# Threshold attention and a SwiGLU block on one core: a weight's conversion in the first batch is parted over two slots, its clamp goes to GpSimd, and the raw places change

## The chip, the cores and the metric

The kernel runs on one core of a Trainium2 chip. The metric is the device time of one execution in microseconds. The engines of the core work side by side, each through a queue of its own in order: PE (TensorE, matmuls), DVE (VectorE), ACT (ScalarE), POOL (GpSimd) and SP (SyncE, which here only issues DMAs). They wait for each other by semaphores.

## What is computed

The reference, cut to what matters:

```python
# q, k, v: (8, 8, 576, 64), tau a scalar
scores = scale * np.matmul(q, k.transpose(0, 1, 3, 2))
thresh = np.max(scores, axis=-1, keepdims=True) - tau
scores = np.where(scores >= thresh, scores, -1000000000.0)
attn = np.exp(scores - np.max(scores, axis=-1, keepdims=True))
attn = attn / (np.sum(attn, axis=-1, keepdims=True) + 1e-09)
x = np.matmul(attn, v)            # then (B,H,S,D) -> (B*S, H*D) = (4608, 512)
g = x @ w_gate                    # (512, 1536)
out = (g * (1 / (1 + np.exp(-g))) * (x @ w_val)) @ w_out
```

The three weights come as 64-bit floats; the kernel makes 32-bit ones of them itself.

## The kernel before, in words

**The stages.** The first batch of the attention is worked on in an order written out by hand (loop of L682): eight segments, each of one pair of heads, first four segments with the tiles 0 and 1 of 128 queries (n = 0 to 3), then four segments with the tiles 2, 3 and 4 (n = 4 to 7; tile 4 is the half tile of 64 queries, and has one maximum, one exponential and one mask instead of two). After it, from `halved` on, come the 7 other batches in slots of a third of a pair of heads; there a planner (`Plan`, with a cost in us for each job and a rank) decides the order on DVE, ACT, POOL and SP, while the order on PE is that of the calls.

**One tile of the first batch.** `scores` is a generator that is stepped from the loop: PE makes the scores (L415, L421), DVE their maxima `nm` (L432), ACT the threshold `th` and the exponential (L435, L436), DVE masks and sums (L439), sums up and inverts (L441, L442 `ri`). Of the two heads of a tile, ACT scales the first (L449) and POOL the second (L447). Between these steps stand the work of the tile before, that is the transposes on PE (L481, L483), their copies on ACT (L489, L493, L496) and the products with v (L513, L516, copy L518), and pieces of the matmuls for the SwiGLU of the first 256 tokens (L530 `pg` and `pv`, with ACT's L545 and L546, DVE's L554 and POOL's product L561). The scores need two PSUM buffers; a tile of two heads takes both, so that the next tile's scores wait for the masks.

**A weight's conversion.** A piece of the weights is 128 x 768 values, 16 pieces of `w_gate` with `w_val` and 8 of `w_out`. SP fetches its raw 64-bit words into a place (L277, L280); there are six places of 6 KB a partition: 0 to 3 in `wo`, 4 in `xall`, 5 in `extra`. Then ACT takes the magnitude of the upper word into the weight's own place (L296) and the lower word into one of three buffers `lo` that take turns (L297); a clamp (L289) follows, a shift by 3 (L310), on DVE the sign by a XOR with the raw upper word (L313, `SCALAR_TENSOR_TENSOR`), and on POOL the addition of `lo` (L315). After L313 and L297 the raw place may be fetched into again. The clamp is on POOL for what is split in the segments n = 0 to 3 (`early_slots`), and on DVE later. In a tile, `split_weights` stands before the masks and `join_weights` (clamp, shift, XOR and addition of the piece split one tile earlier) after `ri`. In the half tile of n = 4 to 6 (`double`), two pieces are joined and a second one is split. `need(n)` forces conversions that a matmul needs at once.

**Where the results lie.** The eight pieces of `w_out` are written into `wo`, on which the places 0 to 3 lie too: the pieces 0 and 1 lie on place 0, the pieces 2 and 3 on place 1, and so on.

**What is left.** The pieces that are not through at the end of the first batch go to the planner by `rest_of_weights` (ACT L834 and L837, DVE L842, L844, L846, POOL L848, SP L825). In the slots, `FIRST_POOLED` says how many scalings POOL does of a slot (L1737 in place of ACT's L1740), and `FIRST_MAX_BY_ACT` in which slots ACT instead of DVE exchanges the halves of the maxima (L1701 in place of L1695).

Of the kernel before, what the change touches and what calls it, by code (L numbers as in the profile page):

```python
# [14 lines left out]
ALU = mybir.AluOpType  # L15
# [97 lines left out]
def kernel(  # L113
# [135 lines left out]
    places = [land[:, n * 2 * TW:(n + 1) * 2 * TW] for n in range(NF * DM // (2 * TW))]  # L249
    places += [xall[:, 3 * XW:3 * XW + 2 * TW], extra[:, 4 * S:4 * S + 2 * TW]]  # L250
    assert 2 * TW == 3 * HW and 4 * S + 3 * TW == 3 * WS and 4 * S + TW == 6 * HW
# [5 lines left out]
    nf = TW // DM2  # L257
    wplaces = deque([1, 4, 2, 5, 3, 4, 5, 4])
    for e in range(2):
# [23 lines left out]
    def words(place, dst, w):  # L283
        return places[place].bitcast(U32).rearrange("p (m n w) -> p m n w", m=dst.shape[1], w=2)[:, :, :, w]

    early_slots, clamped = [True], []

    def clamp(eng, x):
        eng.tensor_scalar(out=x, in0=x, scalar1=1.875 * 2.0 ** -80, scalar2=2.0 ** -111, op0=ALU.min, op1=ALU.max)  # L289

    def split_weights():
        if fetched:
            dst, place = fetched.popleft()
            lo = los[0].rearrange("p (m n) -> p m n", m=dst.shape[1])
            los.rotate(1)
            nc.scalar.activation(dst, words(place, dst, 1).bitcast(F32), AF.Abs, scale=2.0 ** -96)  # L296
            nc.scalar.activation(lo, words(place, dst, 0), AF.Identity, bias=minus2, scale=-2.0 ** -51)  # L297
            if early_slots[0]:
                clamp(nc.gpsimd, dst)
                clamped.append(dst)  # L300
            split.append((dst, place, lo))

    def join_weights(n=1):
        steps = [split.popleft() for _ in range(min(n, len(split)))]
        for up, place, lo in steps:
            if not any(up is x for x in clamped):
                clamp(nc.vector, up)
        for up, place, lo in steps:
            ub = up.bitcast(U32)
            nc.vector.tensor_scalar(out=ub, in0=ub, scalar1=3, scalar2=None, op0=ALU.logical_shift_left)  # L310
        for up, place, lo in steps:
            ub = up.bitcast(U32)
            nc.vector.scalar_tensor_tensor(out=ub, in0=words(place, up, 1), scalar=0x80000000, in1=ub,  # L313
                                           op0=ALU.bitwise_and, op1=ALU.bitwise_xor)
            nc.gpsimd.tensor_tensor(out=ub, in0=ub, in1=lo.bitcast(U32), op=ALU.add)  # L315
            joined.append(up)
            used.discard(place)

    def need(n):
        while len(joined) < n:  # L320
            fetch_weights(2)
            if not split:
                split_weights()
            join_weights()
            split_weights()
# [233 lines left out]
    def gates():  # L559
        for ht, gt in ungated:  # L560
            nc.gpsimd.tensor_tensor(out=ht, in0=ht, in1=gt, op=ALU.mult)  # L561
        ungated.clear()
# [115 lines left out]
    for n, seg in enumerate(segs[:2 * NP]):  # L678
# [3 lines left out]
        for x, t in enumerate(seg["tiles"]):  # L682
            go = scores(seg, t)
            next(go)
            if not n and not x:
                run_idle(6)
# [14 lines left out]
            if n or x:  # L701
                split_weights()
                fetch_weights(2)
            next(go)
            double = t == NT and NP <= n < NP + 3
            if more and not double:
                join_weights()
            fill(part)
            next(go)
            fill(part)  # L710
            if double:
                join_weights(2)
                split_weights()
                fetch_weights(2)
            gates()
# [19 lines left out]

    fill(left[0])
    gates()

# [75 lines left out]
    def rest_of_weights():  # L814
# [3 lines left out]
        done, joins = {}, []  # L818
        for dst, srcs, place, lo in todo:
            m = dst.shape[1]  # L820
            j = None
            if srcs:
                def fetch(dst=dst, srcs=srcs, place=place):
                    to = places[place].bitcast(U64).rearrange("p (m n) -> p m n", m=nf)
                    nc.sync.dma_start(out=to, in_=srcs[0])  # L825

                j = job("SP", 0.1, fetch, done.get(place), lag=5.0)
            if lo is None:
# [9 lines left out]

                j = job("ACT", 0.93, up_part, j, done.get(place), rank=2)
                j = job("ACT", 1.03, lo_part, j, before, rank=2)  # L840
            ub = dst.bitcast(U32)
            j = job("DVE", 0.6, lambda dst=dst: nc.vector.tensor_scalar(  # L842
                out=dst, in0=dst, scalar1=1.875 * 2.0 ** -80, scalar2=2.0 ** -111, op0=ALU.min, op1=ALU.max), j, rank=2)
            j = job("DVE", 0.6, lambda ub=ub: nc.vector.tensor_scalar(  # L844
# [1022 lines left out]
    MAX_BY_ACT = (0, 3, 5, 6, 8, 9, 10)  # L1867
    FIRST_POOLED = {1: 3, 2: 2, 3: 2, 4: 3, 5: 1, 7: 2, 8: 2, 9: 1, 10: 2, 11: 1, 12: 1, 13: 3, 15: 3, 16: 3, 18: 3, 19: 1, 20: 1, 21: 3, 22: 1, 23: 3}
    FIRST_MAX_BY_ACT = (1, 2, 3, 6, 9, 12, 14, 15, 16, 17, 18, 20, 21, 22)
    CD = {0: 1, 1: 1, 9: 2, 10: 2, 11: 2}  # L1870
# [151 lines left out]
```

## Time and profile before

| | |
|---|---|
| median of 5 runs | 1377.68 us (1377.41 to 1378.21) |
| profiled execution, its own time | 1377.02 us |
| its span, first to last instruction | 1374.9 us |
| granted TensorE clock | 1.00 throughout |
| PE busy | 1355.7 us, 99% of the span, 15630 matmuls |
| DVE busy | 1076.3 us, 78% |
| ACT busy | 874.4 us, 64% |
| POOL busy | 708.7 us, 52% |

The profile is of one execution; times in it count from the first instruction of the span, and the profiled execution's own time is 2.1 us longer than its span. A row of the timeline has the start, the length, the engine, the line, the operation and in brackets the idle time ahead of it with what ended it. A busy PE is not PE at its peak, since a matmul that stands in the queue with its weights loaded counts as busy.

### The profile page before, as it was taken

Reading aid. Unit: us, or ns where it says so; the run is one execution under the profiler, and the core shown is the slowest. Engines: PE = TensorE matmul, PEld = TensorE weight load, DVE = VectorE, ACT = ScalarE, POOL = GpSimd, SP = SyncE. Lnnn points to the kernel's source line nnn. Section 1 sums busy time; section 2 is a strip of 40 time slices with the busy share of each in tenths; the row PEclk is TensorE's granted clock in tenths of the full one; section 3 lists DMA queues with packets and bytes.
Section 4 is the critical chain, followed back from the end, with each engine's and each line's share of the span. In section 5 each row is a group of like instructions: output and inputs, shape, how many; then the busy total and the mean of one; then the engine's idle time right before and its main releaser. Section 6 shows DMA issues by size and latency. Waiting matters only on the chain.

```text
span 1374.9 us, 39287 instructions
## 1 busy us (share of the span) xinstructions
PE 1355.7 (99%) x15630; PEld 1117.5 (81%) x15630; DVE 1076.3 (78%) x2822; ACT 874.4 (64%) x2278; POOL 708.7 (52%) x656
## 2 busy tenths in 40 slices
PE   9988999999999999999999999999999999999998
PEld 6766787778778778887888888878887788999998
DVE  6788988887887776787678877877777776787786
ACT  6887766676756767767776766776667764330330
POOL 3566498844474669534974288436943593000000
PEclk9999999999999999999999999999999999999999
DMA  8744413465523541555154523553065404423421
GB/s 176 198 134 136 87 36 100 130 181 143 174 51 123 145 114 41 170 143 143 29 159 129 147 55 123 140 144 94 27 196 148 112 20 143 161 78 138 154 69 32
DMA packets 208295, 162.33 MB, mean 118 GB/s; under 512 B 166128, under 2 KB 180464, under 8 KB 202736
## 3 DMA queue, kind: packets, MB, share of 16 engines
q1 hardware_dynamic: 203920, 158.86, 40.5%
q8 instruction: 124, 2.03, 0.6%
q10 hardware_dynamic: 4192, 0.95, 0.3%
q14 instruction: 59, 0.48, 0.1%
HBM read 138.28 MB, written 21.50 MB: 116 GB/s over the span
## 4 chain that ended last, share of the span: by engine, by line
PE 90%; DVE 4%; ACT 3%; SPq 2%; issue 1%; DMA 1%; ACTq 0%; DVEq 0%
PE pb L954 18%; PE pa L954 12%; PE px L1434 12%; PE sc L1666 10%; PE xa L1763 9%; PE pe L954 9%; PE po L1230 5%; PE py L1443 5%; PE sc L1115 2%; PE pg L1161 2%; PE pv L1161 2%; SPq L344 1%; PE pe L1115 1%; PE sc L1434 1%; PE pv L530 1%
## 5 line engine op out<-in xcount | busy, mean ns | idle before, releaser
L1714 DVE SCALAR_TENSOR_TENSOR pall<-sc,th,pall 128x288 f32<-128x288 f32 x504 | 243.7, 514 | 63.1 <-ACT pall L1712 48.9
L954 PE MATMUL pb<-xall,big 128*128 128x256 f32 x1152 | 273.6, 380 | 0.0
L1712 ACT ACTIVATE pall<-sc,nm 128x288 f32<-128x288 f32 x504 | 231.6, 497 | 34.6 <-DVE pall L1714 34.3
L954 PEld LDWEIGHTS pb<-xall,big 128*128 128x128 f32 x1152 | 216.4, 190 | 31.0 <-issue 2.2
L1742 DVE STREAM_TRANSPOSE pall<-pall 128x576 f32<-128x576 f32 x252 | 189.9, 765 | 59.2 <-ACT pall L1740 42.6
L1740 ACT ACTIVATE pall<-pall,ri 128x288 f32<-128x288 f32 x408 | 186.6, 527 | 25.0 <-DVE ri L1728 24.3
L809 POOL TENSOR_TENSOR hall<-hall,tmp 128x512 f32<-128x512 f32 x80 | 103.6, 1295 | 159.7 <-DVE hall L1007 144.3
L954 PE MATMUL pa<-xall,big 128*128 128x256 f32 x768 | 183.4, 382 | 0.0
L954 PEld LDWEIGHTS pa<-xall,big 128*128 128x128 f32 x768 | 143.1, 190 | 22.0 <-issue 3.1
L1666 PE MATMUL sc<-kT,qT 64*32 64x144 f32 (+1 forms) x5376 | 149.5, 346 | 3.0 <-DVE pall L1714 2.2
L1687 DVE TENSOR_REDUCE mx<-sc 128x2 f32<-128x576 f32 x168 | 124.7, 742 | 27.2 <-PE sc L1666 26.7
L1666 PEld LDWEIGHTS sc<-kT,qT 64*32 64x32 f32 x5376 | 98.4, 106 | 56.4 <-issue 20.8
L954 PE MATMUL pe<-xall,big 128*128 128x256 f32 x576 | 137.3, 381 | 0.0
L1763 PE MATMUL xa<-pall,vall 64*32 64x288 f32 x4032 | 132.2, 404 | 1.0 <-DVE hall L1007 0.8
L1737 POOL TENSOR_SCALAR pall<-pall,ri 128x288 f32<-128x288 f32 x96 | 95.7, 1009 | 63.4 <-DVE ri L1728 63.3
L954 PEld LDWEIGHTS pe<-xall,big 128*128 128x128 f32 x576 | 108.5, 190 | 16.9 <-issue 2.7
L1763 PEld LDWEIGHTS xa<-pall,vall 64*32 64x32 f32 x4032 | 76.4, 107 | 50.1 <-issue 7.2
L1722 ACT COPY sums<-sums 32x6 f32<-32x6 f32 x336 | 66.6, 198 | 45.1 <-DVE pall L1714 40.5
L1701 ACT COPY mx<-mx 32x6 f32<-32x6 f32 x196 | 38.1, 194 | 61.2 <-DVE mx L1689 59.2
L1006 ACT ACTIVATE vall<-tmp 128x512 f32<-128x512 f32 x96 | 60.1, 629 | 23.3 <-POOL tmp L809 9.6
L1443 PE MATMUL py<-wo,hall 128*128 128x256 f32 x336 | 74.8, 379 | 0.0
L1689 DVE TENSOR_REDUCE mx<-sc 128x1 f32<-128x288 f32 x168 | 74.6, 444 | 0.0
(257 smaller groups left out, 2471.5 us busy)
## 6 DMA issues: line engine op xcount, KB each, us to landing
big<-sums_hbm SPq DMA_DIRECT2D x42, 1024.0 KB, 5.2
big<-sums_hbm SPq DMA_DIRECT2D x48, 768.0 KB, 4.7
vall<-in_v_dram SPq DMA_DIRECT2D x112, 144.0 KB, 3.0
out_dram<-big SPq DMA_DIRECT2D x32, 256.0 KB, 3.1
qT<-in_q_dram SPq DMA_DIRECT2D x112, 72.0 KB, 4.6
kT<-in_k_dram SPq DMA_DIRECT2D x112, 72.0 KB, 2.9
wo<-in_moe_w_gate_dram SPq DMA_DIRECT2D x16, 384.0 KB, 3.7
wo<-in_moe_w_val_dram SPq DMA_DIRECT2D x16, 384.0 KB, 4.6
```

The lines of the kernel that those rows point to most:

```text
L809: return lambda: nc.gpsimd.tensor_tensor(out=out, in0=a, in1=b, op=op)
L954: nc.tensor.matmul(ps[:, i], w[:, k_, i * P:(i + 1) * P], x[:, k_, :], start=first and i == k_ == 0, stop=True, skip_group_check=True)
L1434: nc.tensor.matmul(ps, a[:, f, :], ws[n][:, f, :], start=bank_ not in begun, stop=True, skip_group_check=True)
L1443: nc.tensor.matmul(ps(), a[:, f, i * P:(i + 1) * P], operands[o][:, f, :], start=first and f == 0, stop=True, skip_group_check=True)
L1666: nc.tensor.matmul(pss[h][(slice(g * G, (g + 1) * G), *part)], qT[hs, col:col + G], kT[hs, c * SH + keys[0]:c * SH + keys[1]], start=True, ...
L1687: rs.append(job("DVE", 0.72, lambda n=n, tile_=tile_: nc.vector.tensor_reduce(out=mx[:, n:n + 2, 0], in_=tile_[:, :, 0:SH], axis=AX.X, op= ...
L1712: ej = job("ACT", 0.42, lambda x=x, n=n: nc.scalar.activation(ps[x], scs[x], AF.Exp, bias=nm[:, n:n + 1]), ej, *((masks[h, 0], masks[h, 1] ...
L1714: masks[x] = job("DVE", 0.45, lambda x=x, n=n: nc.vector.scalar_tensor_tensor(out=ps[x], in0=scs[x], scalar=th[:, n:n + 1], in1=ps[x], op0 ...
L1737: scaled.append(job("POOL", 1.02, lambda x=x, n=n: nc.gpsimd.tensor_scalar(out=x, in0=x, scalar1=ri[:, n:n + 1], scalar2=None, op0=ALU.mul ...
L1740: scaled.append(job("ACT", 0.46, lambda x=x, n=n: nc.scalar.activation(x, x, AF.Copy, scale=ri[:, n:n + 1]), rj, rank=rank))
L1742: seg["turned"].append(job("DVE", 0.72, lambda both=both: nc.vector.transpose(out=both, in_=both), *scaled, rank=rank))
L1763: nc.tensor.matmul(holds[a].ap()[x * G:(x + 1) * G, 0:SH].rearrange("d (i q) -> d i q", q=G), vr[rs, h, j, ds], p[rs, h, :, j, :], start=( ...
```

## The change

The conversion of a piece is cut in two. `shift_weights` stands where `join_weights` stood and does the shift only; the XOR and the addition (`join_weights`) come in the next tile, behind its maxima. The clamp is always POOL's: in n = 4 to 7 it stands behind POOL's scaling (`clamp_split`), for the first four segments directly behind the split as before. A seventh place, in `hall`, is added, and the pieces of `w_out` use the places 6, 4, 5, 3, 4, 5, 4, 5 instead of 1, 4, 2, 5, 3, 4, 5, 4. At the end of the first batch one more piece is joined and one more is fetched. In `rest_of_weights` a piece that lies on a place waits for what was read there (`under`), and a piece that is clamped already isn't clamped again. The two tables for the slots of the second batch have new entries; the number of POOL's scalings in them is 41 in both, of them in the slots 0 to 8 now 18 instead of 15, and ACT's exchanges of maxima go from 14 to 12 (slot 0 is now one of them).

```diff
-    places += [xall[:, 3 * XW:3 * XW + 2 * TW], extra[:, 4 * S:4 * S + 2 * TW]]
+    places += [xall[:, 3 * XW:3 * XW + 2 * TW], extra[:, 4 * S:4 * S + 2 * TW], h1all[:, 0:2 * TW]]
...
-    wplaces = deque([1, 4, 2, 5, 3, 4, 5, 4])
+    wplaces = deque([6, 4, 5, 3, 4, 5, 4, 5])
...
+            unclamped.append(dst)
             if early_slots[0]:
-                clamp(nc.gpsimd, dst)
-                clamped.append(dst)
+                clamp_split()
             split.append((dst, place, lo))
 
-    def join_weights(n=1):
+    def clamp_split():
+        while unclamped:
+            dst = unclamped.popleft()
+            clamp(nc.gpsimd, dst)
+            clamped.append(dst)
+
+    def shift_weights(n=1):
+
         steps = [split.popleft() for _ in range(min(n, len(split)))]
-        for up, place, lo in steps:
-            if not any(up is x for x in clamped):
-                clamp(nc.vector, up)
+        if any(up is x for up, place, lo in steps for x in unclamped):
+            clamp_split()
         for up, place, lo in steps:
             ub = up.bitcast(U32)
             nc.vector.tensor_scalar(out=ub, in0=ub, scalar1=3, scalar2=None, op0=ALU.logical_shift_left)
-        for up, place, lo in steps:
+        shifted.extend(steps)
+
+    def join_weights():
+        for up, place, lo in shifted:
             ub = up.bitcast(U32)
             nc.vector.scalar_tensor_tensor(out=ub, in0=words(place, up, 1), scalar=0x80000000, in1=ub,
                                            op0=ALU.bitwise_and, op1=ALU.bitwise_xor)
             nc.gpsimd.tensor_tensor(out=ub, in0=ub, in1=lo.bitcast(U32), op=ALU.add)
             joined.append(up)
             used.discard(place)
+        shifted.clear()
...
             go = scores(seg, t)
             next(go)
+            join_weights()
...
             next(go)
+            clamp_split()
             double = t == NT and NP <= n < NP + 3
             if more and not double:
-                join_weights()
+                shift_weights()
             fill(part)
             next(go)
             fill(part)
             if double:
-                join_weights(2)
+                shift_weights(2)
                 split_weights()
+                clamp_split()
                 fetch_weights(2)
             gates()
...
     fill(left[0])
+    join_weights()
+    fetch_weights()
     gates()
...
+            under = done.get((NW // 3 - len(todo) + n) // 2)
...
-                j = job("ACT", 0.93, up_part, j, done.get(place), rank=2)
+                j = job("ACT", 0.93, up_part, j, done.get(place), under, rank=2)
...
-            j = job("DVE", 0.6, lambda dst=dst: nc.vector.tensor_scalar(
-                out=dst, in0=dst, scalar1=1.875 * 2.0 ** -80, scalar2=2.0 ** -111, op0=ALU.min, op1=ALU.max), j, rank=2)
+            if not any(dst is x for x in clamped):
+                j = job("DVE", 0.6, lambda dst=dst: clamp(nc.vector, dst), j, rank=2)
...
-    FIRST_POOLED = {1: 3, 2: 2, 3: 2, 4: 3, 5: 1, 7: 2, 8: 2, 9: 1, 10: 2, 11: 1, 12: 1, 13: 3, 15: 3, 16: 3, 18: 3, 19: 1, 20: 1, 21: 3, 22: 1, 23: 3}
-    FIRST_MAX_BY_ACT = (1, 2, 3, 6, 9, 12, 14, 15, 16, 17, 18, 20, 21, 22)
+    FIRST_POOLED = {0: 3, 1: 1, 2: 2, 3: 2, 4: 3, 5: 1, 6: 2, 7: 2, 8: 2, 10: 2, 11: 1, 12: 1, 14: 2, 15: 2, 16: 3, 17: 2, 18: 2, 19: 3, 20: 1, 22: 2, 23: 2}
+    FIRST_MAX_BY_ACT = (0, 3, 6, 9, 12, 14, 15, 16, 18, 20, 21, 22)
```

More of the change, by code (lines that the diff above doesn't have):

```diff
@@ L284, in words @@
         return places[place].bitcast(U32).rearrange("p (m n w) -> p m n w", m=dst.shape[1], w=2)[:, :, :, w]
-    early_slots, clamped = [True], []
+    early_slots, clamped, unclamped, shifted = [True], [], deque(), []
     def clamp(eng, x):
@@ L317, in join_weights @@
             used.discard(place)
+        shifted.clear()
     def need(n):
+        if len(joined) < n:
+            join_weights()
         while len(joined) < n:
@@ L704 @@
             next(go)
+            clamp_split()
             double = t == NT and NP <= n < NP + 3
             if more and not double:
-                join_weights()
+                shift_weights()
             fill(part)
@@ L736 @@
     fill(left[0])
+    join_weights()
+    fetch_weights()
     gates()
@@ L818, in rest_of_weights @@
         done, joins = {}, []
-        for dst, srcs, place, lo in todo:
+        for n, (dst, srcs, place, lo) in enumerate(todo):
             m = dst.shape[1]
             j = None
+            under = done.get((NW // 3 - len(todo) + n) // 2)
             if srcs:
```

## The prediction

> **What bounds the kernel.** First the share of busy time: PE 99%. Then the order of the instructions: PE runs the same 7861 instructions in the same order before and after, so the time can only change by PE's pauses. Then PE's waits in the first 170 us (engine, line, what it waited for, us in total, times, longest):
>
> ```profile
> PE tp L481 <- ACT tmp L546: 4.9, 4, 1.4
> PE sc L415 <- DVE pall L439: 3.4, 4, 1.5
> PE sc L1666 <- DVE pall L1714: 1.6, 1, 1.6
> ...
> PE tp L481 <- POOL pall L447: 0.5, 1, 0.5
> ```
>
> They add up to 10.4 us; behind 161 us PE's pauses come to about 2 us. What can be won lies between 57 and 161 us. There the table by stretches (length, busy us of PE, PEld, DVE, ACT, POOL, clock, DMA) shows a period of three tiles, from one L481 of the second tile to the next:
>
> ```profile
> 70.57:91.86 21.29, 18.76 (x146) 14.08 (x146) 18.77 (x37) 17.67 (x35) 14.59 (x9) 1.00 0.45 150
> 91.86:113.16 21.30, 18.76 (x147) 14.09 (x147) 18.45 (x35) 17.67 (x35) 12.99 (x8) 1.00 0.54 185
> 113.16:134.43 21.27, 18.71 (x146) 14.08 (x147) 18.04 (x35) 17.62 (x35) 12.98 (x8) 1.00 0.23 75
> ```
>
> No engine is full. The chain of waits (start, us, what) says what the period is made of:
>
> ```profile
> 95.26 0.69 DVE hall L554
> 95.95 0.94 DVE big L289 x2
> ...
> 97.74 1.82 DVE big L313 x2
> 99.56 0.68 DVE nm L432
> ...
> 103.25 1.42 DVE big L289
> ...
> 104.69 0.99 DVE big L310
> ...
> 105.71 0.96 DVE big L313
> 106.67 0.68 DVE nm L432
> ```
>
> DVE's conversions stand ahead of the maxima twice in a period; the rest of it is ACT's row from `th` to L546.
>
> **The change in one period.** I count from 91.86, the start of L481 of the second tile. Before: L554 at 3.4, two clamps, shifts, XORs to 7.7, maxima of the first tile 7.6 to 9.0, masks 9.4 to 11.0, its conversion 11.3 to 14.8, maxima of the second tile 14.7, `th` 15.5, L546 ends at 21.24, L481 at 21.3. POOL: two L315 7.0 to 11.1, L561 to 12.4, L447 to 14.39; the second half of L481 of the first tile follows at 14.44.
>
> After: the clamps leave DVE (0.94 for the pair, 1.49 and 0.54 for the single ones), so the shifts run 4.0 to 5.0 and the maxima 4.95 to 6.3. The two XORs follow there, 6.3 to 8.2, and cost little on DVE: ACT's `th` and exponential (0.29 and 0.64 in the chain) cover the first. Masks 8.2 to 9.8, `ri` 10.2, scores of the second tile at 9.65 instead of 10.33. DVE is no longer the bound.
>
> POOL takes its place. Its queue is now clamp, clamp, L561, L315, L315, L447. What two-input work on both engines does to each other, the timeline shows:
>
> ```profile
> 98.84 2.39 POOL L315 TENSOR_TENSOR big<-big,extra 128x768 uint32<-128x768 uint32 x1 [5.27 <-DVE big L313]
> ...
> 102.97 1.27 POOL L561 TENSOR_TENSOR hall<-hall,tmp 128x512 f32<-128x512 f32 x1
> 103.17 1.49 DVE L289 TENSOR_SCALAR big<-big 128x768 f32<-128x768 f32 x1
> ...
> 104.23 2.02 POOL L447 TENSOR_SCALAR pall<-pall,ri 128x576 f32<-128x576 f32 x1
> 104.69 0.98 DVE L310 TENSOR_SCALAR big<-big 128x768 uint32<-128x768 uint32 x1
> ```
>
> The addition, begun in the second XOR, took 2.39 instead of the 1.81 of its neighbours: it waited for the XOR's end. DVE's clamp, begun in L561, took 1.49 instead of 0.54: it waited for L561's end. So these exclude each other, while a shift beside the scaling L447 only slows from 0.54 to 0.98.
>
> The second clamp waits for L296 (end at 5.7) and takes 0.83 to 1.04, so that L561 is ready at 6.7, when the first XOR has just begun. If L561 waits out both XORs: 8.2 + 1.28 + 1.81 + 1.81 + 1.95 = 15.05. If it comes between them: 7.3 + 1.28, the second XOR to 9.45, then 1.81 + 1.81 + 1.95, 15.0. If DVE's shift gets between the additions, 0.4 more. If L561 comes first (in the first period a scaling of q, 1.72 us, is ahead of the clamps and delays the maxima): 6.33 + 1.28, XORs to 9.4, additions to 12.8, L447 to 14.85. From the second half of L481 to the next L481, PE has 5.42 us without a pause (106.30 to the end of L516 at 111.72). Periods of 14.85 to 15.45 + 5.42 = 20.3 to 20.9, against 21.3. I take 20.35, 20.5 and 20.5: **2.55 us less in three periods**. The bounds: without any exclusion L447 would end at 13.7 and the period be 19.2, 2.1 less each; the other end is in the rivals.
>
> The Trainium skill (SBUF — State Buffer, Who interferes with whom) says of the pair of ports that VectorE and GpSimd share that whoever comes second waits for the whole instruction, also VectorE's fast one-input forms against any GpSimd operation: against this change, since it puts more on GpSimd. The rows agree for two-input work, but not for a shift beside the scaling, which took 0.98. By the rule the shift of the second tile would wait for the whole scaling, push `th` of the half tile, the clamps and L561 by some 0.7 us a period (an estimate by that page), and the sum would end about 2 us higher.
>
> **What else moves.** In the first eight tiles, PE stands in a row from 42 to 57 us, and the XOR (0.96) fits into DVE's pause ahead of the masks (0.74 to 0.88) and the time won ahead of the maxima: nothing, except 0.2 us at 27 us, where the maxima no longer wait for the XOR. POOL's clamps there stay where they are. L313 also frees the raw place: SP's fetch now starts some 0.5 us later in a period (100.1 for 99.64), and its data are split 10 us later; behind it on SP stand only fetches. L297 of the first tile waits for the addition three pieces back (11.3 instead of 9.9): L449 ends at 13.1, before POOL's half. The other places take away ACT's idle 2.08 us at 118.0, but that period is 21.27 like the others, so it was covered: nothing.
>
> **The passage to the slots** is where I see a new wait. The last piece but one now lies in place 4 (`xall`); its fetch waits for the last XOR of the first batch, which stands behind L554. From L481 at 0 (134.43 before): L554 to 4.95, delayed by the shift that meets an addition, XOR to 5.9, fetch. It lands 4.2 to 4.7 us later (112.95 to 117.12, 134.26 to 138.96), or longer by the medians of these transfers (KB, us to landing):
>
> ```profile
> wo<-in_moe_w_out_dram SPq DMA_DIRECT2D x3, 768.0 KB, 4.4
> xall<-in_moe_w_out_dram SPq DMA_DIRECT2D x3, 768.0 KB, 5.1
> ```
>
> Before, that piece was fetched at 134.26 and split at 142.40, position 8.0, without a wait. Now L834 can start at 10.7. It blocks what is behind it in ACT's queue: L837, ACT's exchange of the maxima (0.8, new in slot 0), `th`, the exponentials; DVE's last clamp and the minimum wait too. `th` comes at 13.6 instead of 9.7, the masks that free the scores' buffer end at 16.9, the next slot's scores start at 17.05 instead of 14.59: 2.4 us of new wait. In that slot DVE (masks' end 17.3, then 0.5 + 0.95 + 0.35 + 0.65 + 0.75 + 2.05 + 0.65 + 0.2) reaches `th` at 23.6, and by the 4.03 us from `th` to the next scores before (156.25 to 160.28) those start at 27.6 instead of 25.85. That includes the old wait of 1.57. **1.7 us more** (1.0 to 2.6 by the landing). Eight loads of q and k stand behind the fetch on SP, to 13.6; kT is needed at 19.9.
>
> The tables of the slots: the same 41 scalings, three more of 1.0 us in the slots 0 to 8, where POOL was full from 180 to 220 us. PE did not wait for POOL there, and the output's sums are needed only from about 235 us. Nothing, between -1 (the pauses left) and +1.
>
> **Sum**: -0.2 - 2.55 + 1.7 = -1.05 against the profiled execution's own 1377.02, that is 1376.0. The runs' median, 1377.68, is 0.66 above that: **1376.6**.
>
> **Rivals.**
> - *POOL gets through*: the clamps are done earlier or the exclusion is milder, 19.2 a period: -6.3 - 0.2 + 1.7 = -4.8, **1372.9**. For it: in the first tile of a period nothing but a quarter of a us decides whether L561 meets the XORs. Against: POOL is then busy over 17 us of 19.
> - *POOL's row becomes longer than the old bound* (slower): the place is L447 of the first tile. Its price is one for one as soon as it ends later than 21.3 - 5.42 = 15.88. If an addition takes 2.39 and the shift gets between, 16.3: +0.42 x 3 - 0.2 + 1.7 = +2.8, **1380.5**. For it: the additions that meet an XOR did take 2.39. Against: the masks that now run beside them read only one input from SBUF.
> - *PE is full anyway*: PE's own work in a period is 21.3 less its pauses (0.65, 0.51, 1.37) and less the 0.8 by which the second tile's scores are drawn out (2.13 for 1.36), 18.0 us; this binds only below all these times.
>
> **Chances.** Forecast 0.41, first rival 0.37, second 0.22. The bound for faster and slower is 0.2%, 2.75 us, about what a measurement of this kernel can tell from no change. The first rival lies beyond it, the second just: faster 0.37, same 0.42, slower 0.21. The range reaches to both, 1372.4 to 1380.5; the forecast's own is 1375.0 to 1378.5.
>
> **What would show it.** The period of L481: 20.3 to 20.9 (19.2 the first rival, over 21.3 the second); L481 waiting for L447 instead of L546; L561 or an XOR of 1.6 us and more beside each other; ACT idle ahead of L834 for some 2.5 us with a DMA as its end, and the slot's scores waiting for L1714 by more than 2 us. If PE waits for POOL's sums behind 180 us, my last term is wrong.

## The result, and the profile after

The changed kernel takes **1375.64 us** (median of 27 runs, 1373.37 to 1379.31) against 1377.69 us of the kernel before (45 runs): a ratio of 0.9983, 95% interval 0.9978 to 0.9989, so 2.05 us less. The forecast was 1376.6, which is 1.1 us less than before; the measured median is another 1.0 us lower. The profiled execution took 1376.36 us, its span is 1374.3 us (1374.9 before), and its granted clock 0.998 (1.0 before).

Most line numbers behind L247 have moved; those met most, old and new: shift L310, now L316; XOR L313, L322; addition L315, L324; scores L415, L428; masks L439, L452; scaling L447, L460; transposes L481, L494; L546, L559; value L554, L567; product L561, L574; the split in the slots L834, L853; the slots' scores L1666, L1685 and masks L1714, L1733. The clamp stays L289.

PE's waits of the changed kernel in the first 170 us (engine, line, what it waited for, us in total, times, longest):

```profile
PE tp L494 <- POOL pall L460: 3.3, 3, 1.1
PE sc L428 <- DVE pall L452: 2.7, 4, 1.3
PE sc L1685 <- DVE pall L1733: 2.2, 2, 1.9
PE sc L428 <- DVE qT L657: 1.9, 1, 1.9
...
PE tp L494 <- ACT tmp L559: 1.2, 1, 1.2
```

ACT's 4.9 us ahead of the transposes have shrunk to 1.2, and POOL's scaling stands in their place, as forecast. The slots' scores wait 2.2 us instead of 1.6. The table by stretches shows the period, here from one second half of L494 to the next (length, busy us of PE, PEld, DVE, ACT, POOL, clock, DMA):

```profile
86.53:106.65 20.12, 18.63 (x147) 14.03 (x147) 17.37 (x31) 17.59 (x35) 18.17 (x12) 1.00 0.58 197
106.65:126.75 20.10, 18.20 (x145) 13.64 (x145) 17.36 (x31) 17.60 (x35) 18.14 (x12) 1.00 0.25 79
```

20.1 us instead of 21.3. POOL went from 13 or 14.6 us of 21.3 to 18.2 of 20.1: it is the fullest engine beside PE, whose 18.2 to 18.6 include what stands in the queue.

Laid side by side, the same PE instructions of both profiled executions say where the time went. PE's order is the same, so a difference of starts is a sum of pauses and clock:

| PE instruction, time before | after less before, us | step |
|---|---|---|
| scores at 73.86 | +1.37 | +1.37 in the early tiles |
| slot 0's scores, 137.72 | -1.83 | -3.20 in three periods |
| slot 2's scores, 160.28 | -1.05 | +0.78 in the passage |
| a product at 194.01 | -1.56 | -0.51 in the slots |
| the end | -0.62 | +0.94 behind 450 us, in steps of 0.1 to 0.6 |

The forecast had -0.2, -2.55, +1.7 and 0: a sum near the measured one, out of four terms that are each off by 0.5 to 1.6 us. That is what the experiments are about. The last row is of this one execution: in seven of the twelve profiles below the step behind 450 us is 0.2 us or less either way, in the other five 0.3 to 2.2 us later, and its cause stays open.

### The profile page after: what moved, and what is told of

Read it like the earlier page. It is cut to its first block, busy times and chain, and to the rows that moved or that the text cites. A ratio compares the mean times of both kernels' runs of the same rounds, so it can differ in the third digit from the quotient of the medians.

```text
span 1374.3 us, 39266 instructions
## 1 busy us (share of the span) xinstructions
PE 1355.1 (99%) x15630; PEld 1114.0 (81%) x15630; DVE 1073.3 (78%) x2815; ACT 873.4 (64%) x2270; POOL 725.4 (53%) x671
## 3 DMA queue, kind: packets, MB, share of 16 engines
q8 instruction: 124, 2.03, 0.6%
HBM read 138.28 MB, written 21.50 MB: 116 GB/s over the span
## 4 chain that ended last, share of the span: by engine, by line
PE 91%; ACT 2%; DVE 2%; SPq 1%; POOL 1%; DMA 1%; issue 1%; ACTq 0%; DVEq 0%; POOLq 0%
PE pb L973 18%; PE pa L973 12%; PE px L1453 12%; PE sc L1685 10%; PE xa L1782 9%; PE pe L973 9%; PE po L1249 5%; PE py L1462 5%; PE sc L1134 2%; PE pg L1180 2%; PE pv L1180 2%; SPq L357 1%; PE pe L1134 1%; PE sc L1453 1%; PE pv L543 1%
## 5 line engine op out<-in xcount | busy, mean ns | idle before, releaser
L1733 DVE SCALAR_TENSOR_TENSOR pall<-sc,th,pall 128x288 f32<-128x288 f32 x504 | 243.9, 514 | 62.8 <-ACT pall L1731 48.4
L1685 PE MATMUL sc<-kT,qT 64*32 64x144 f32 (+1 forms) x5376 | 150.0, 345 | 3.9 <-DVE pall L1733 2.8
L1685 PEld LDWEIGHTS sc<-kT,qT 64*32 64x32 f32 x5376 | 97.3, 106 | 58.9 <-issue 19.3
L827 POOL TENSOR_TENSOR tmp<-tmp 128x512 f32<-128x512 f32 x36 | 45.9, 1275 | 60.2 <-ACT tmp L1048 60.2
```

The costliest lines, as they stand in the source:

```text
L827: return lambda: nc.gpsimd.tensor_tensor(out=out, in0=a, in1=b, op=op)
L1685: nc.tensor.matmul(pss[h][(slice(g * G, (g + 1) * G), *part)], qT[hs, col:col + G], kT[hs, c * SH + keys[0]:c * SH + keys[1]], start=True, ...
L1733: masks[x] = job("DVE", 0.45, lambda x=x, n=n: nc.vector.scalar_tensor_tensor(out=ps[x], in0=scs[x], scalar=th[:, n:n + 1], in1=ps[x], op0 ...
```

## Experiments

Each kernel is the changed one with the edit shown, except where another is named. "From slot 0 to slot 2" is the time between the starts of these slots' scores, and "a period" the time between the scores of the first tiles of two following segments; both are of the profiled execution.

**The first eight tiles as before.**

```diff
             if more and not double:
                 shift_weights()
+                if n < NP:
+                    join_weights()
```

> The changed kernel, but in the first eight tiles (segments 0 to 3) sign and addition follow the shift at once, as before the change; from segment 4 on they stay behind the next maxima. Theory: the changed kernel loses 1.1 to 1.4 us up to the scores at 41.57 us, because the addition L324, now begun beside the next tile's scores (34.87 to 36.70), makes the next shift L316 wait for its end (2.18 us instead of 0.54), and the XOR L322 then stands ahead of the masks. So here no shift before 57 us takes over 0.6 us, the wait of 1.30 us ahead of the scores at 41.57 falls to about 0.2, and the total is 1.2 us lower than the changed kernel's, about 0.9974 of the kernel before. Rival: the loss comes from the arrival of the first q (PE's first wait was 1.86 us for 0.78) and has nothing to do with the edit: then a wait of over 1 us stays before 60 us and the total is that of the changed kernel, 0.9983.

Measured: 1375.68 us, 0.9982 (0.9973 to 0.9990). In its profile the wait ahead of the scores near 41 us is 0.47 us instead of 1.30 (some 0.2 expected), the longest shift before 57 us takes 0.80 us instead of 2.18 (0.6 expected), and the scores at 73.86 come at 74.03, +0.17 instead of +1.37. So the first part of the theory holds, its two sizes a little low, and the rival falls: this execution had a long first wait for q as well (1.48 us) and kept no loss from it. The total says nothing: both expectations lie in its interval. This profile lost 1.7 us elsewhere, by a clock drop that is told of below.

What happens at 35 us is in the timeline of the changed kernel (start, length, engine, line):

```profile
34.87 1.83 POOL L324 TENSOR_TENSOR big<-big 128x768 uint32<-128x768 uint32 x1
...
34.94 2.18 DVE L316 TENSOR_SCALAR big<-big 128x768 uint32<-128x768 uint32 x1
```

The shift begins 0.07 us into the addition, and takes 2.18 us instead of 0.54: it waits for the addition's end at 36.70. Behind it stand the transposes of k and q and the maxima, and then the XOR of 0.93 us ahead of the masks. But this needs the two to meet. In the run with the deferred product, further down, whose instructions are the same up to there, q landed 0.7 us later (29.99 for 29.32), GpSimd's queue shifted, the scaling of q (L361) stood beside the shift instead of the addition, and it was the scaling that took longer (1.49 for 1.08):

```profile
34.12 1.49 POOL L361 TENSOR_SCALAR hall<-hall,scl 128x320 f32<-128x320 f32 x1
...
34.18 0.56 DVE L316 TENSOR_SCALAR big<-big 128x768 uint32<-128x768 uint32 x1
```

Over the profiles, the PE instruction at 54.74 us of the kernel before comes +1.34, +1.46 (less its clock drop), +1.64, +0.77 and -0.34 us later in the five kernels with the late XOR there, and +0.13 to +0.32 in five with the early one. The late XOR costs 0.8 us more than the early one on the mean there, and it depends on the transfers.

**A free place for the last piece but one.**

```diff
-    wplaces = deque([6, 4, 5, 3, 4, 5, 4, 5])
+    wplaces = deque([6, 4, 5, 3, 4, 5, 6, 5])
```

> The changed kernel, but the last piece of w_out but one lies in the place in hall that the first piece of w_out has long left, so that its fetch waits for no XOR. Theory: the wait at the passage to the slots is this fetch: ACT's idle time of 2.05 us ahead of L853 goes, PE's wait of 1.89 us ahead of the scores at 148.84 falls under 0.3; the next slot's wait comes back to some 1.0 to 1.6 (0.27 now), so that slot 0's to slot 2's scores take 22.5 us (23.34 now, 22.56 in the kernel before) and the total falls by 0.8 us, to 0.9977 of the kernel before. Rival: masks and conversions on DVE hold the scores' buffers anyway: ACT's idle time goes but PE's wait stays over 1.5 us, and the total is that of the changed kernel, 0.9983.

Measured: 1374.38 us, 0.9970 (0.9958 to 0.9982). First the passage in the timeline of the changed kernel, from the last XOR to the wait:

```profile
136.61 0.98 DVE L322 SCALAR_TENSOR_TENSOR wo<-xall,wo 128x768 uint32<-128x768 uint32 x1
...
137.66 0.37 SPq L277 DMA_DIRECT2D xall<-in_moe_w_out_dram  x1
...
142.43 0.91 ACT L853 ACTIVATE wo<-xall 128x768 f32<-128x768 f32 x1 [2.05 <-DMA xall<-in_moe_w_out_dram]
...
148.84 0.67 PE L1685 MATMUL sc<-kT,qT 64*32 64x288 f32 x2 [1.89 <-DVE pall L1733]
```

The XOR frees the place at 137.59, the fetch is issued at 137.66 and lands 4.8 us later, ACT stands idle for 2.05 us, and PE's next scores wait for 1.89 us. With the free place, PE's waits from 140 to 170 us are one line:

```profile
PE sc L1685 <- DVE pall L1733: 0.3, 1, 0.3
```

From slot 0 to slot 2 it takes 21.19 us instead of 23.34. The rival falls, and the theory is short: the wait was worth 2.15 us, not 0.8, since the old wait of 1.57 us ahead of slot 2's scores did not come back. Something else in the change had taken it away.

**The old tables.**

```diff
-    FIRST_POOLED = {0: 3, 1: 1, 2: 2, 3: 2, 4: 3, 5: 1, 6: 2, 7: 2, 8: 2, 10: 2, 11: 1, 12: 1, 14: 2, 15: 2, 16: 3, 17: 2, 18: 2, 19: 3, 20: 1, 22: 2, 23: 2}
-    FIRST_MAX_BY_ACT = (0, 3, 6, 9, 12, 14, 15, 16, 18, 20, 21, 22)
+    FIRST_POOLED = {1: 3, 2: 2, 3: 2, 4: 3, 5: 1, 7: 2, 8: 2, 9: 1, 10: 2, 11: 1, 12: 1, 13: 3, 15: 3, 16: 3, 18: 3, 19: 1, 20: 1, 21: 3, 22: 1, 23: 3}
+    FIRST_MAX_BY_ACT = (1, 2, 3, 6, 9, 12, 14, 15, 16, 17, 18, 20, 21, 22)
```

> The changed kernel with the two tables of the kernel before (which slot's scalings GpSimd takes, in which slots ACT exchanges the maxima). Theory: the new tables take away the old wait of 1.57 us ahead of slot 2's scores (0.27 in the changed kernel, though its wait one slot earlier is 1.89), and this is why the passage cost 0.78 us and not the 1.7 of the forecast; so with the old tables PE waits 1.0 to 1.8 us ahead of slot 2's scores, slot 0's to slot 2's scores take 24.0 to 24.6 us (23.34 with the new ones), the total is some 1 us higher, 0.9990 of the kernel before. Rival: the tables do nothing here, and the old wait went because the slots start from other times of the transfers: 23.2 to 23.5 from slot 0 to slot 2, total 0.9983.

Measured: 1380.57 us, 1.0011 (1.0003 to 1.0020): with the old tables the changed kernel is slower than the kernel before. From slot 0 to slot 2 it takes 25.40 us, and PE's waits from 60 to 240 us have

```profile
PE sc L1685 <- DVE pall L1733: 5.4, 3, 2.9
```

1.36 us ahead of slot 1, 2.86 ahead of slot 2, and 1.22 at 225 us. The difference to the changed kernel is 2.1 us from slot 0 to slot 2, and 2.1 more by 233 us. By the ratios it is 3.9 us (1.0011 against 0.9983). Tables that only say which engine does what are worth more here than the three periods together (3.2).

**The new tables alone, in the kernel before.** The diff is the last one turned round, on the kernel before:

```diff
-    FIRST_MAX_BY_ACT = (1, 2, 3, 6, 9, 12, 14, 15, 16, 17, 18, 20, 21, 22)
+    FIRST_MAX_BY_ACT = (0, 3, 6, 9, 12, 14, 15, 16, 18, 20, 21, 22)
...
```

> The kernel before with nothing but the two new tables. With the changed kernel they were worth 2.1 us from slot 0's to slot 2's scores (25.40 us with the old ones, 23.34 with the new) and some 1.6 us more up to 233 us. Theory: they suit these slots in any case, so here too the wait of 1.57 us ahead of slot 2's scores goes: 21.0 to 21.5 us from slot 0 to slot 2 (22.56 with the old ones), total 0.9985 to 0.9992. Rival: they only suit the changed kernel, whose slots start with other transfers and a late weight: 22.3 to 23.5 here, total 0.9997 to 1.001.

Measured: 1386.30 us, 1.0059 (1.0045 to 1.0073), far beyond both expectations. From slot 0 to slot 2 it takes 23.2 us, no better than with the old ones, and one wait at 184 us is longer than all others:

```profile
PE xa L1763 <- ACT sums L1722: 4.8, 1, 4.8
```

The theory that the tables suit the slots in any case falls. The tables feed a planner, and what it makes of them depends on the rest of its jobs: in the kernel before, its list has one clamp more for DVE (the changed kernel's comes already clamped), and it puts shifts and XORs of that conversion between the slot's masks. Which of this makes the wait of 4.8 us is not shown: no run takes it apart. Two clock drops of 3.4 us, of the kind told of below, add to this profile.

**The clamps on DVE again**, from segment 4 on.

```diff
-        if any(up is x for up, place, lo in steps for x in unclamped):
-            clamp_split()
+        for up, place, lo in steps:
+            if any(up is x for x in unclamped):
+                clamp(nc.vector, up)
+                clamped.append(up)
+                unclamped.remove(up)
...
             next(go)
-            clamp_split()
             double = t == NT and NP <= n < NP + 3
...
                 split_weights()
-                clamp_split()
                 fetch_weights(2)
```

> The changed kernel, but from segment 4 on the clamps stand on DVE ahead of the shifts again; sign and addition stay behind the next maxima. Theory: the two parts of the change each carry some of the 1.2 us that a period of three tiles became shorter (21.3 to 20.1), and the clamps carry most: with two clamps (0.94 us) ahead of the maxima again, and DVE's clamp held up by the product L574, which no longer waits behind POOL's clamps, the XORs end about 1 us later, and POOL's row behind them with L460 too: a period of 20.7 to 21.0, the total 2 to 2.5 us over the changed kernel's, 1.0000 of the kernel before (0.9993 to 1.0005). Rival: the clamps don't matter, since moving the XORs and additions behind the maxima is what shortens a period: 20.1, and the total of the changed kernel, 0.9983.

Measured: 1394.00 us, 1.0113 (1.0099 to 1.0127). Both expectations miss the total, and not for the clamps' own time. This kernel has the new tables with a clamp left for the slots, as the last one had, and the same wait of 4.8 us stands at 191 us:

```profile
PE xa L1783 <- ACT sums L1742: 4.8, 1, 4.8
```

Three clock drops of 6.8 us each stand in this profile as well. So its total tells nothing of a period. Its periods do: 21.89 and 21.50 us (the third has a clock drop in it). That is more than the 20.7 to 21.0 of the theory, and more than the 21.3 of the kernel before: the moved XORs and additions, without the clamps' move, lose 0.2 to 0.6 us a period. DVE's clamp now is the one that begins in an addition, 2.10 us for 0.54, and the shift and the maxima stand behind it.

**Sign and addition at once behind the shift, everywhere.**

```diff
             if more and not double:
                 shift_weights()
+                join_weights()
...
                 shift_weights(2)
+                join_weights()
```

> The changed kernel, but sign and addition follow the shift at once everywhere, so that only the clamps' move to POOL, the new places and the tables are left of the change. By the forecast's rules: POOL's queue is then addition, addition, clamp, L574, L460 and ends about 14.4 us behind L494 of the second tile, no later than now (14.6), but the second tile's shift has to wait for a clamp that stands behind two additions and then for L574: its maxima start at about 14 for 14.7 in the kernel before, and ACT's row brings L494 at 20.3 to 20.7. A period of 20.3 to 20.7, no loss in the first eight tiles, the fetch at the passage leaves a period earlier and brings no wait: total 0.998 to 0.9988 of the kernel before. Rival: the XORs' move carries the gain, and without it a period stays at 21.2 to 21.4: total 0.9995 to 1.0003. Other rival: the clamps alone carry it all: 20.1 or less a period, and with neither loss the total is 0.997 or less.

Measured: 1375.67 us, 0.9982 (0.9973 to 0.9991). Periods of 20.68, 20.57 and 20.54 us, and no early loss (+0.17), as expected. The clamps' move, with the new places that this kernel keeps, thus brings 2.07 of the 3.20 us that the three periods lost, the XORs' move on top of it 1.13; without the clamps' move the XORs' lost, so the two don't add up one by one. No run has the new places alone. The last part of the expectation fell: the fetch was issued at 137.34, 0.07 us behind the last XOR, and slot 1's scores waited 1.52 us. The late fetch needs the new order of the places and not the late XORs.

**The same with the free place.** To the last diff comes

```diff
-    wplaces = deque([6, 4, 5, 3, 4, 5, 4, 5])
+    wplaces = deque([6, 4, 5, 3, 4, 5, 6, 5])
```

> The changed kernel with sign and addition at once behind the shift everywhere, and the last piece of w_out but one in hall: left of the change are the clamps on GpSimd, the free place and the tables. The run with the joins at once still had the late fetch (issued at 137.34, right behind the last XOR), so the passage's wait comes from the order of the places and not from the moved XORs. Theory: it goes here too, PE waits under 0.3 us ahead of slot 1's scores (1.52 there), slot 0 to slot 2 takes 21.0 to 21.5 us (22.96 there); a period stays at 20.55, so that this kernel is 1.2 to 1.5 us above the one with both losses out: 0.996 to 0.9965. Rival: the moved XORs are worth nothing once their losses are out: 0.9948 to 0.9956, like that kernel.

Measured: 1373.95 us, 0.9970 (0.9959 to 0.9982). From slot 0 to slot 2 21.19 us, as expected. Of its periods, 20.73, 21.39 and 20.55, the second holds a clock drop. The total lies above the 0.9960 to 0.9965 expected, which is inside the interval, and above the rival's 0.9948 to 0.9956, which is outside. So the moved XORs seem worth something once their losses are out; the totals say it weakly, since this interval overlaps that of the kernel with both losses out (0.9939 to 0.9964, below), and the 1.13 us of the periods say it better.

**The product of the double tiles deferred.**

```diff
-            gates()
+            if not double:
+                gates()
             last = go
```

> The changed kernel, but in the three tiles whose conversion takes two weights at once the product L574 isn't issued there; it goes out at the end of the next tile, behind that tile's scaling L460 and clamp in GpSimd's queue. Theory: a period of 20.1 us is GpSimd's row clamp, L574, two additions, L460 and DVE's XORs that L574 splits (the first XOR and L574 and the second XOR follow each other, 118.35 to 121.24). Without L574 between them the second XOR ends 1.1 us earlier, so do the masks and L460, PE's wait of 1.11 us for L460 and its wait of 0.37 to 0.80 us for the masks both go, and the second tile's L460 comes 1.3 us later against its own tile, with about 1.1 us to spare: a period of 19.0 to 19.5, the total 2 to 3 us under the changed kernel's, 0.9965 of the kernel before. Rival: GpSimd's queue has no room in the next tile either, and PE waits for that tile's L460 instead: a period of 19.9 to 20.2 and the total of the changed kernel, 0.9983.

To see why, the chain of waits of the changed kernel at the third period (start, us, what):

```profile
117.64 0.83 POOL wo L289
118.47 1.96 POOL hall L574
120.42 2.73 POOL wo L324 x2
...
124.67 2.03 POOL pall L460
126.70 0.04 issue
126.75 0.66 PE tp L494 x4
```

L574 is 1.96 us here because it waits for the first XOR's end (119.29) and the second XOR then waits for its end (120.42). Measured: 1374.53 us, 0.9975 (0.9964 to 0.9985), periods of 20.33, 19.54 and 19.55 us. PE's waits from 60 to 240 us:

```profile
PE tp L494 <- POOL pall L460: 4.0, 5, 1.1
```

Five waits instead of three: the masks' wait is gone, that of the first tile is still 1.1 us, and two of 0.33 us are new, for the second tile's L460. The last two periods are 0.6 and 1.0 us shorter, just beyond the upper end of the theory, the first 0.3 longer, and the total lies between both expectations, which are both in its interval. The mechanism holds in one half: the exclusion was in the row. PE now waits for POOL's scaling in both tiles, but POOL's queue isn't full: from 84.67 to 104.20 us it is busy for 16.8 of 19.5 us, and it stands idle for 1.41 us until ACT's L296 and for 1.31 us until the XOR. What bounds the period is the row of DVE's XORs, the two additions and the scaling, which follow each other there from 96.85 to 104.15 us.

**Both losses out, without and with the deferral.** The edits of the first two experiments together, then with the last:

```diff
             if more and not double:
                 shift_weights()
+                if n < NP:
+                    join_weights()
...
-    wplaces = deque([6, 4, 5, 3, 4, 5, 4, 5])
+    wplaces = deque([6, 4, 5, 3, 4, 5, 6, 5])
...
-            gates()
+            if not double:
+                gates()
```

> The changed kernel with two edits that were tried alone: in the first eight tiles sign and addition follow the shift at once, and the last piece of w_out but one lies in hall. Theory: the two losses are separate, 1.2 us at 41 us and 2.15 us at the passage (slot 0's to slot 2's scores 21.2 instead of 23.34), and the first was hidden in the median of its own run only by clock drops behind PE's pause of 1.98 us at the passage, which is gone here: 3.0 to 3.6 us under the changed kernel, 0.9955 to 0.9962 of the kernel before. Rival: what is won in the first eight tiles isn't kept (its run alone was no faster than the changed kernel's): then the total is that of the kernel with the free place, 0.9970.

> The changed kernel with both edits and the product L574 of the three double conversions deferred to the next tile. If a period falls to 19.2 us by the deferral, 2 to 3 us under the kernel with the two edits alone: 0.9935 to 0.9945 of the kernel before. If GpSimd's queue holds the next tile instead, no difference from that kernel: 0.9955 to 0.9962.

Measured: 1372.19 us, 0.9952 (0.9939 to 0.9964), and 1371.86 us, 0.9947 (0.9934 to 0.9959). Both beat the changed kernel. In the first the scores at 73.86 come +0.22, slot 0 to slot 2 takes 21.17 us, and all PE instructions behind 194 us stand 4.8 us earlier than before, so the two losses are separate and kept. Its five runs lie within 0.7 us. Part of what it gains over the kernel with the free place alone (1374.38 us) are clock drops: four of that kernel's runs have a mean granted clock of 1.00 and took 1371.14 to 1373.92 us, the other four have 0.997 or 0.998 and took 1374.84 to 1377.00, and all five here have 1.00. The second has a second and third period of 19.53 us, but the totals of the two can't be told apart.

**Pauses made on purpose.** Fills of a constant on DVE (they compute nothing) ahead of the masks of the first tile of segments 1 to 7, in the kernel with both losses out:

```diff
             flips = flip_steps()
+            if not x:
+                for _ in range((0, 6, 7, 8, 9, 10, 12, 14)[n]):
+                    nc.vector.memset(ones, 1.0)
```

> The changed kernel with both losses out, and with idle work on VectorE ahead of the masks in the first tile of segments 1 to 7 (6, 7, 8, 9, 10, 12, 14 fills of a constant, some 0.27 us each, that compute nothing), which makes TensorE wait there: pauses from 0.5 to 3.5 us, growing. Theory: in nine profiles every stretch at half clock (3.4 us long, a loss of 1.7 us) began within 2 us of the end of a pause of 1.29 us or more, and about one such pause in three had one; so drops here come behind the pauses over 1.3 us only, more of them behind the longest, 2 to 5 in all. Rival: the drops are chance and have nothing to do with pauses: none or one, also where TensorE did not pause.

> The same with the fills in the other order (14, 12, 10, 9, 8, 7, 6), so that the long pauses stand in other tiles and at other times. Theory: the drops move to the first segments, behind the pauses over 1.3 us. Rival: they stand where they stood, whatever the length of the pause ahead of them, or there are none.

Measured, one execution each: 1395.19 and 1400.20 us. The pauses that came of it are longer than meant (0.45 to 6.05 us). Growing: no drop behind 1.31 us and less, one behind each of 3.96, 4.73 and 6.05. Falling: a drop behind each of 2.64, 2.45, 1.67, 3.17, 2.88 and 2.85 us, and behind a first wait for q of 1.85. The rival of chance falls. In the falling order every pause made is longer than 1.6 us, so the drops stand in all segments and not in the first ones alone, as had been expected. The table by stretches of the second kernel, behind the pause of 1.67 us that ended at 58.22 (the third number from the end is the clock):

```profile
52.00:58.00 6.00, 4.55 (x42) 3.37 (x40) 4.76 (x16) 5.80 (x14) 3.76 (x4) 1.00 0.80 186
...
61.00:64.00 3.00, 3.00 (x23) 2.34 (x23) 0.98 (x2) 0.36 (x3) 2.60 (x2) 0.50 0.65 201
...
67.00:70.00 3.00, 3.00 (x33) 2.15 (x33) 2.41 (x4) 2.67 (x5) 1.04 (x2) 1.00 0.19 27
```

## Why the prediction came out right, and which steps did not

**The period: mechanism right, size a little short.** The forecast let POOL's row clamp, clamp, L561, L315, L315, L447 take over as the bound, with L481 waiting for L447; this is what PE's waits show, 1.1 us each time. It let L447 end 14.85 to 15.05 us behind L481 of the second tile; in the third period it ends 14.7 us behind it (112.01 to 126.70). The row is shorter because the lengths were added up whole, while each instruction here follows the end of the one before by less than its own length: in the third period L574 1.13 of 1.28, the second XOR 0.82 of 0.95, the first addition 1.67 of 1.81. So the three periods lost 3.20 us instead of 2.55. The first rival, that POOL gets through (19.2 a period), is out: L574 did meet the XORs in the second and third period (2.03 and 2.00 us in the timeline, for 1.28); in the first it ran ahead of them (1.27), and the row still ended 14.5 us behind. The second rival needed L447 to end later than 15.88; an addition did take 2.5 us beside an XOR, but the shift did not get between the additions. It began in the second one and waited (2.10 us), so it delayed DVE and not POOL.

**The Trainium skill's rule on the shared ports** (SBUF — State Buffer, Who interferes with whom) is seen beside the additions: the shift waited for the whole of the rest. Beside a scaling of one input it is not: in the prediction's row the shift, begun 0.46 us into the scaling of 2.02 us, took 0.98 us and ended before it. The shift of 0.56 us above went through too, while POOL's instruction took the longer, but the two began within 0.06 us, so that row alone doesn't tell which had come first. The 0.7 us a period that the rule would have added does not show: the row ended earlier than the sum without it.

**The first eight tiles: the step failed.** "The XOR (0.96) fits into DVE's pause ahead of the masks": PE waits for the masks in one tile only, 1.30 us at 41.57. What the step left out is that the addition moves with the XOR, into the time of the next tile's shift, and that what was weighed in the late tiles (a shift that gets between additions) holds here too. It cost 1.4 us in this execution and 0.8 on the mean of five, where the forecast won 0.2.

**The passage: the wait was right, the sum was not.** ACT idle for 2.05 us with a DMA as its end (forecast some 2.5), the fetch landing after 4.8 us (4.2 to 5.1), and the scores waiting 1.89 us (2.4) came as described. But the forecast kept the old wait of 1.57 us behind it; it fell to 0.27. With the old tables it did not fall, and the passage then costs 25.40 - 22.56 = 2.84 us, more than the forecast's range of 1.0 to 2.6: the term of 1.7 was too small for the fetch, and too large only because the new tables won. (Its sum for DVE in that slot, from 17.3 on, adds up to 23.4 and not to 23.6.) And of the two things that it named for the late fetch, place 4 and the XOR's new position behind L554, the place is enough: the run with early joins still waits for 1.52 us.

**The tables: the step failed by the most.** "Nothing, between -1 and +1" counted scalings, and looked for POOL's sums as what could go wrong; behind 170 us PE has no wait for POOL. The tables decide an order that the planner writes, and with the old ones the passage and the slots cost 4.4 us (from slot 0 to 233 us) where the new ones cost 0.3. Without this the changed kernel would have been on the other side, 1.0011.

**The sum** was near by luck: an early loss of 1.4 us that it did not have stands against 0.65 us more won in the periods and 1.4 us less lost from slot 0 to 194 us. The median fell by more than the pair of profiles says (2.05 for 0.66 us): the profiled execution of the changed kernel lies 0.7 us above its median, with 0.94 us lost late, and that of the kernel before 0.7 us below its own.

## What to carry over

When an instruction is moved, move everything behind it in the account: here the addition on the other engine, which then met the next shift, mattered more than the XOR that was moved. Where a planner decides an order from tables, an edit of a table, or of one job in its list, must be priced by looking at the order that comes out, since the number of operations says nothing of it. And a forecast whose total is right should still be held against the stages: here four terms cancelled, which is luck.

## What the hardware did that was not expected

TensorE's granted clock can halve behind a pause of 1.3 to 2 us. One such stretch, in the kernel with the first tiles as before, behind its pause of 1.98 us that ended at 147.75:

```profile
146.00:148.00 2.00, 0.25 (x1) 0.14 (x2) 1.80 (x7) 1.84 (x6) 1.02 (x1) 1.00 0.83 205
148.00:150.00 2.00, 2.00 (x40) 1.19 (x45) 1.93 (x7) 1.34 (x6) 0.27 (x1) 0.60 0.53 201
150.00:152.00 2.00, 2.00 (x53) 1.53 (x37) 1.92 (x4) 0.00 (x0) 2.00 (x2) 0.55 0.00 0
152.00:154.00 2.00, 2.00 (x16) 1.72 (x13) 1.93 (x7) 1.56 (x5) 2.00 (x3) 1.00 0.04 9
```

In stretches of half a us the clock reads 0.50 from 148.4 to 151.8: 3.4 us at half speed, a loss of 1.7 us. In all fourteen profiles of this study, outside the last 20 us of a span, each drop stands at or behind a pause of at least 1.29 us, and it lasts 3.4, 6.8 or 10.2 us, so one to three such stretches. Of 30 pauses from 1.29 to 2.0 us 8 had a drop, of 12 longer ones 11, and of some hundred pauses from 0.4 to 1.28 us none (PE's wait of 1.31 us ahead of its first matmul, the same in every profile and without a drop, isn't counted).

The starts of the drops tell more. Within a profile they lie whole steps of 3.413 us apart: in the kernel with the falling pauses at 28.40, 42.05, 59.12, 100.08, 123.97 and 147.86 us, that is 4, 5, 12, 7 and 7 steps. So the clock changes on a fixed grid, which lies differently in each profile, and a pause can be cut by it. Counted by these steps, as long as the clock was full, all 13 steps in which PE was idle for 1.85 us or more were followed by half clock, 5 of 22 with 1.28 to 1.81 us, and one shorter one, which holds the second part of a pause of 2.64 us. The one pause over 2 us without a drop (2.86 us, with the old tables) is cut by its grid into 1.59 and 1.28 us. What decides between 1.28 and 1.81 us stays open.

The changed kernel's own first wait of 1.86 us had one (from 7.5 to 11 us), which the waits behind it took up: at 33.6 us PE's order is only 0.19 us behind that of the kernel before. The Trainium skill (TensorE: Matmul & The Clock Gate, HAM oscillation — how this bites in real kernels) gives a window of about 3.4 us and warns of idle gaps longer than that. The length of a stretch agrees; idle gaps far shorter than that were enough here, from 1.29 us on.

So a new pause of 1.9 us is worth more than its length on the mean, and a kernel with such pauses has runs that lie far apart. Every run's mean granted clock is on record, and the times go with it: of the changed kernel's 27 runs the 15 with 1.00 took 1373.37 to 1375.95 us (mean 1374.71), the 9 with 0.999 had a mean of 1376.41, and the slowest, with 0.996, took 1379.31. The five runs of the kernel with both losses out have 1.00 and lie within 0.7 us. One pause can be enough for the spread: the kernel with the free place spreads over 5.9 us, and in its profile the one pause of 1.29 us or more is that of 1.29 us at 41.67, with a drop behind it.
